# Sixteen small softmax operations of an attention and MLP kernel get a choice of engine, with a new order of the work

## The chip, the cores and the metric

The kernel runs on one core of a Trainium2 chip. The core has five engines that work side by side, each through its own queue in order: TensorE (PE, matrix multiplications and transposes), VectorE (DVE), ScalarE (ACT), GpSimd (POOL) and SyncE (SP), which here only issues transfers. The metric is the device time of one execution in microseconds (us), lower is better.

## The reference

Attention in two parts for 8 batches, 8 heads, 576 positions, 64 channels each, and then an MLP over all 4608 tokens. One part attends within a band of 7 positions, the other between averages of 4 positions; their outputs are added.

```python
q_d = q.reshape(B, H, S // 4, 4, D).mean(axis=3)        # and k_d, v_d alike
out_d = softmax_attention(q_d, k_d, v_d)                # exp(s - max) / (sum + 1e-9)
out_up = np.repeat(out_d, 4, axis=2)
scores = np.where(abs(i - j) < 4, scale * q @ k.T, -1e9)
out_local = softmax(scores) @ v                         # the same 1e-9 beside the sum
x = (out_up + out_local).transpose(0, 2, 1, 3).reshape(B * S, H * D)
h = np.maximum(np.maximum(x @ w1, x @ w2), x @ w3)      # 512 -> 768
return h @ w_out                                        # 768 -> 512
```

Every softmax has two small steps beside its large ones: the maximum is scaled and negated before it goes into the exponential, and 1e-9 is added to the sum before the reciprocal.

## The kernel before, in words

The MLP is most of the work. Its float32 products are made of three TensorE products each: every operand is split into a high part (names in `hi`) and the rest (names in `lo`), and high by high, high by low and low by high are summed. The weights come in six slices of the hidden layer (`whi0`, `wlo0` to `whi5`, `wlo5`, made by `weight_in`), w_out in six parts (`weight_out`). A batch of 512 tokens takes `mlp_in`, which goes through the six slices, and `mlp_out`.

Attention is done by half-batches `n` of four heads. The last 16 pooled positions of each batch are collected as a ninth block. From the third batch on, attention (`block`) runs beside the MLP of earlier batches, mostly on VectorE, ScalarE and GpSimd. For the first two batches (`n` from 0 to 3, the set `DENSE`) there is no MLP to run beside, and `dense` computes the band on TensorE too, in these steps for each half-batch:

- `q`, `v`: loads; `qk` (`pooled_qk`): sums of four positions, `hp` and `qkT` in the profile.
- `s0`, `s1` (`band_scores`): for two heads at a time, scores over windows of 70 positions, a maximum `mx`, eight exponentials on ScalarE that also leave their sums in `z`, then 1e-9 added to `z`, its reciprocal, and the multiplication (`sm`; for n=1 it lies in a tile lent by a weight, `whi`).
- `tail`, `vd`: pooled values (`traw`, `vtail`, `hv`, `vd`).
- `sums` (`pooled_scores`): pooled scores, maximum and its scaling in `nz` (first half, `nm`), six exponentials into `pd` with sums in `nz` (second half, `zd`), 1e-9 added, reciprocal `rd`, multiplication; then `ptld` collects the last positions, TensorE transposes the weights, and copies bring them to `pt` and `ptt`. For n=1 `pd` is lent too and appears as `wlo`.
- `pv`: pooled output (`od`); `v0`, `v1` (`band_values`): TensorE transposes the band weights, copies `y`, 32 products with the values, and the sum with `od` into `t`, which is then split into `xhi` and `xlo` for the MLP.

Nothing of this is issued where it stands in the code. Every operation is recorded (class `Recorder`), with the engines that may take it. `place` then orders all of them: at each turn it takes the engine that can begin first, and on it, among the operations that are ready, the one of smallest priority. Priorities come from tables: `PLAN` for the steps of `dense`, by engine where it matters, `WLOAD` and `WMAKE` for the weights, `WOUT` for w_out, `BEGIN` for the first steps of the fifth half-batch. `HOMES` is a table of letters that ties single copies, multiplications and casts to ScalarE (A) or VectorE (D); "-" leaves the choice to `place`. `emit` issues the result, each engine's list in its order, so all rows of the profile carry its line, L495, and are told apart by their tiles. PSUM has eight banks in two sets, `pm` (three) and `pa` (five); the tile `t` has three buffers, the raw halves of the weights (`hh`, `wo`) two each.

In the kernel before, the two small steps are VectorE's everywhere.

Of the kernel before, what the change touches and what calls it, by code (L numbers as in the profile page):

```python
# [13 lines left out]
AF = mybir.ActivationFunctionType  # L14
# [4 lines left out]
B, H, S, D = 8, 8, 576, 64  # L19
# [11 lines left out]
EPS = 1e-9  # L31
# [1 line left out]
VBUFS = 3  # L33
LAG = 200.0
TAGS = ('pm', 'pm', 'pa', 'pa')
WLOAD = (450.0, 580.0, 2390.0, 260.0, -1745.0, 515.0)
WMAKE = ({"DVE": 1850.0, "ACT": 1125.0}, {"DVE": 560.0, "ACT": -60.0}, {"DVE": 3695.0, "ACT": -1485.0}, {"DVE": 6945.0, "ACT": -1720.0}, {"DVE": 355.0, "ACT": -140.0}, {"DVE": 15.0, "ACT": 40.0})
WOUT = {"DVE": 60.0, "ACT": 2015.0, "SP": 1935.0}
PLAN = (
    (  # L40
        ("q", 0, -2480.0),
        ("v", 0, 905.0),
        ("qk", 0, -2340.0),
        ("s0", 0, {"PE": 1990.0, "DVE": 540.0, "ACT": 1780.0}),
        ("s1", 0, {"PE": -1905.0, "DVE": 65.0, "ACT": 1135.0}),
        ("tail", 0, {"DVE": -405.0, "SP": 480.0}),
        ("q", 1, -975.0),
        ("v", 1, 1150.0),
        ("sums", 0, {"PE": -1675.0, "DVE": -1840.0, "ACT": 260.0}),
        ("vd", 0, {"DVE": -1715.0, "SP": 740.0}),  # L50
        ("qk", 1, -130.0),
        ("s0", 1, {"PE": 15.0, "DVE": -1045.0, "ACT": 1125.0}),
        ("s1", 1, {"PE": 1165.0, "DVE": 235.0, "ACT": 315.0}),
        ("tail", 1, {"DVE": 3360.0, "SP": 2255.0}),
        ("pv", 0, {"PE": -430.0, "ACT": 3475.0}),
        ("v0", 0, {"PE": 195.0, "DVE": -280.0, "ACT": 80.0}),
        ("v1", 0, {"PE": 1795.0, "DVE": 10.0, "ACT": -795.0}),
        ("sums", 1, {"PE": 1905.0, "DVE": 95.0, "ACT": -60.0}),
        ("vd", 1, 3095.0),
        ("pv", 1, {"PE": 95.0, "ACT": 6225.0}),  # L60
        ("v0", 1, {"PE": 1800.0, "DVE": -1230.0, "ACT": 3665.0}),
        ("v1", 1, {"PE": 1685.0, "DVE": 2800.0, "ACT": 1870.0}),
    ),
    (
        ("q", 0, 165.0),
        ("v", 0, -2485.0),
        ("qk", 0, 910.0),
        ("s0", 0, {"PE": 1930.0, "DVE": 60.0, "ACT": 230.0}),
        ("s1", 0, {"PE": 1090.0, "DVE": 1560.0, "ACT": 1425.0}),
        ("tail", 0, {"DVE": 2970.0, "SP": 60.0}),  # L70
        ("sums", 0, {"PE": 820.0, "DVE": -605.0, "ACT": -1890.0}),
        ("vd", 0, {"DVE": -1505.0, "SP": -115.0}),
        ("pv", 0, {"PE": 5.0, "ACT": -1935.0}),
        ("v0", 0, {"PE": 940.0, "DVE": -250.0, "ACT": 1640.0}),
        ("v1", 0, {"PE": 635.0, "DVE": 1895.0, "ACT": 510.0}),
        ("q", 1, 1775.0),
        ("v", 1, 0.0),
        ("qk", 1, -550.0),
        ("s0", 1, {"PE": 615.0, "DVE": -3215.0, "ACT": 130.0}),
        ("s1", 1, {"PE": 225.0, "DVE": 5265.0, "ACT": 485.0}),  # L80
        ("tail", 1, {"DVE": -240.0, "SP": 250.0}),
        ("sums", 1, {"PE": -210.0, "DVE": -120.0, "ACT": 445.0}),
        ("vd", 1, {"DVE": 4855.0, "SP": 1435.0}),
        ("pv", 1, {"PE": -1915.0, "ACT": -2420.0}),
        ("v0", 1, {"PE": 645.0, "DVE": -120.0, "ACT": -85.0, "SP": 6135.0}),
        ("v1", 1, {"PE": 880.0, "DVE": -1450.0, "ACT": 385.0, "SP": 1665.0}),
# [11 lines left out]
DENSE = tuple(range(2 * BANDED))  # L98
# [54 lines left out]
ENGINES = ("PE", "DVE", "ACT", "POOL", "SP")  # L153
DONE_NS = {"PE": 230.0, "DVE": 150.0, "ACT": 190.0, "POOL": 200.0}
MUL_BIAS = {'DVE': 3000.0}
HOMES = {"norm": "AA-A--A-", "band": "A-AADA-AAD-AA---", "hi": "-DAAAAADA-AA", "xhi": "--AA-AAA", "od": "AA--", "pt": "DAAA", "late": "--A-"}
WHEN = {}
PATIENCE = {"PE": 0.0, "DVE": 0.0, "ACT": 0.0, "POOL": 0.0, "SP": 0.0}
LANES = 8
RUN_NS = 200.0  # L160
COLD_US = 35.0
BEGIN = {"PE": 775.0, "DVE": 1695.0, "ACT": 255.0, "POOL": 1095.0, "SP": 510.0}
LAYER_TAGS = {f"{t}{i}" for t in ("whi", "wlo") for i in range(NFT)} | {f"{t}{c}" for t in ("xhi", "xlo") for c in range(NCC)} | {"wo", "hh"}


# [347 lines left out]
def local_global_attention_maxout_kernel(ctx: ExitStack, tc: tile.TileContext, qk_d, qke_d, vw_d, vt_d, wi_d, wo_d, v, ident_d, mask_d, diag_d, band_d, out):  # L513
# [23 lines left out]
    def care(n):  # L537
        return None if n in DENSE else CARE["near" if n < NEAR else "far"]
# [40 lines left out]
    nm, zd = nz[:, 0], nz[:, 1]  # L579
# [60 lines left out]
    def weight_in(ft):  # L640
# [65 lines left out]
    def pooled_scores(n):  # L706
# [7 lines left out]
                    pe.matmul(sps[i][cs, r], qkT[pp, 0, pr, tok : tok + QT], qkT[pp, 1, pr], start=True, stop=True, tile_position=(64 * i, QT * half), skip_group_check=True)  # L714
        for i in range(2):
            dve.tensor_reduce(out=nm[:, i::2], in_=sps[i], axis=AX.X, op=ALU.max)
        dve.tensor_scalar_mul(nm, nm, -1.0 / 128.0)
        pd = st["pd"] if n == 1 else new([P, 6, SD5], tag="pd", name=f"pd_{n}")
        for x in range(6):
            act.activation(pd[:, x, :SD], sps[x % 2][:, x // 2], AF.Exp, bias=nm[:, x : x + 1], scale=1.0 / 128.0, accum_out=zd[:, x : x + 1])  # L720
        dve.tensor_scalar_add(zd, zd, EPS)
        rd = new([P, 6], tag="rd", name=f"rd_{n}")
        dve.reciprocal(rd, zd)

# [5 lines left out]
        pt = st["pt"] = new([P, HH, SD], tag="pt", name=f"pt_{n}")  # L730
# [159 lines left out]
    def band_scores(n, pr, tag):  # L890
        sps = window_scores(n, (pr,), tag, True)[pr]
        if n == 1:
            if pr == 0:
                state[n]["sms"] = guest(n, "sms", "whi4")
            w = 2 * FAC * KWIN
            sm = state[n]["sms"][:, w * pr : w * pr + w].rearrange("p (i u x) -> p i u x", i=2, u=FAC)
        else:
            sm = new([P, 2, FAC, KWIN], tag="sm", bufs=2, name=f"sm_{n}_{pr}")
        mx = new([P, 2, FAC], tag="mx", bufs=2, name=f"mxb_{n}_{pr}")
        z = new([P, 2, FAC], tag="z", bufs=2, name=f"zb_{n}_{pr}")  # L900
        for i in range(2):
# [226 lines left out]
```

## Time and profile before

| | |
|---|---|
| median of 3 runs | 722.41 us (720.45 to 723.44) |
| profiled execution | 720.9 us, its span 719.1 us |
| TensorE busy | 687.1 us, 96% of the span |
| VectorE busy | 533.2 us, 74% |
| ScalarE busy | 400.8 us, 56% |
| GpSimd busy | 184.1 us, 26% |
| mean granted TensorE clock | 0.985 of full |

The span runs from the first to the last instruction of the profiled execution; its own time is 1.8 us longer. "PE MATMUL pm<-xhi_0r,whi_0r" is a TensorE product that writes a bank of `pm` from the tiles behind the arrow. A row of the timeline has start and duration in us, the engine and the operation, and in square brackets how long the engine had stood idle before it and whose result ended that. Where rows are grouped, the last figures are busy us, mean ns of one, and idle time ahead with what ended it. The work of `dense` and of the weights lies in the first 136 us; from 57 us on TensorE has matmuls of the MLP.

### The profile page before, as it was taken

The numbers are of one execution on the slowest core, as the hardware profiler recorded it, in microseconds if no ns is written. First come the engines' busy times: TensorE is split into PE (matmuls) and PEld (weight loads), VectorE is DVE, ScalarE is ACT, GpSimd is POOL, SyncE is SP. The second block draws the span as 40 slices with busy tenths as digits, with TensorE's granted clock in tenths as the row PEclk, the third lists the DMA queues.
The fourth block names the chain that finished last, engine by engine and source line by source line (L and its number), as shares of the span: only waits on it lengthen the run. The fifth ranks groups of instructions, "written<-read, shape, count | busy, mean of one in ns | idle before, by whom it ended". The sixth has DMA issues, their size and how long they took to land.

```text
span 719.1 us, 13533 instructions
## 1 busy us (share of the span) xinstructions
PE 687.1 (96%) x4756; PEld 555.2 (77%) x4756; DVE 533.2 (74%) x952; ACT 400.8 (56%) x1434; POOL 184.1 (26%) x250
## 2 busy tenths in 40 slices
PE   3679999999999999999999999999999999999996
PEld 2557777788878888888888888888888788888885
DVE  6989999887979688869887988796968687431220
ACT  4787774584738283928393739372948387221111
POOL 0000100062415061606150625060605156000000
PEclk9859999999999999999999999999999999999999
DMA  9952717465856677574848684758487673210002
GB/s 361 306 189 84 270 40 219 92 151 139 175 136 191 120 128 185 143 164 81 229 124 187 117 209 113 181 106 184 120 197 130 136 150 78 51 59 30 0 1 58
DMA packets 190817, 101.35 MB, mean 141 GB/s; under 512 B 161454, under 2 KB 166605, under 8 KB 189981
## 3 DMA queue, kind: packets, MB, share of 16 engines
q1 hardware_dynamic: 190749, 100.49, 56.4%
q8 instruction: 37, 0.61, 0.4%
q14 instruction: 31, 0.25, 0.1%
HBM read 71.23 MB, written 29.23 MB: 140 GB/s over the span
## 4 chain that ended last, share of the span: by engine, by line
PE 86%; DVE 7%; DMA 3%; ACT 2%; issue 1%; SPq 0%; ACTq 0%; DVEq 0%
PE pm L495 78%; PE pa L495 8%; DVE pvb L495 1%; DMA pvb<-in_wo_dram 1%; DMA wlo<-in_qk_dram 1%; DVE t L495 1%; DVE hh L495 1%; DVE nz L495 1%; DVE hp L495 1%; SPq L495 0%; DMA t<-xd 0%; DVE xlo_0r L495 0%; ACT pvb L495 0%; DVE mx L495 0%; ACT whi L495 0%
## 5 line engine op out<-in xcount | busy, mean ns | idle before, releaser
L495 PE MATMUL pm<-xhi_0r,whi_0r 128*128 128x512 f32 x648 | 253.9, 392 | 1.5 <-DVE t L495 1.5
L495 PE MATMUL pm<-xlo_0r,whi_0r 128*128 128x512 f32 x648 | 253.4, 391 | 0.0
L495 PE MATMUL pm<-xhi_0r,wlo_0r 128*128 128x512 f32 x648 | 253.3, 391 | 0.0
L495 POOL TENSOR_TENSOR pvb<-v,s 128x256 f32<-128x256 f32 x205 | 161.6, 820 | 203.7 <-DVE s L495 87.3
L495 ACT ACTIVATE pvb<-v,s 128x64 f32<-128x64 f32 x748 | 186.7, 342 | 7.8 <-DMA v<-in_v_dram 3.9
L495 PEld LDWEIGHTS pm<-xhi_0r,whi_0r 128*128 128x128 f32 x648 | 121.6, 188 | 27.7 <-DVE t L495 1.9
L495 PEld LDWEIGHTS pm<-xhi_0r,wlo_0r 128*128 128x128 f32 x648 | 121.7, 188 | 25.8 <-issue 0.6
L495 PEld LDWEIGHTS pm<-xlo_0r,whi_0r 128*128 128x128 f32 x648 | 121.7, 188 | 25.7 <-issue 0.8
L495 DVE TENSOR_TENSOR t<-pm,t 128x512 f32<-128x512 f32 x108 | 74.0, 685 | 81.7 <-PE pm L495 78.7
L495 DVE TENSOR_TENSOR pvb<-pvb 128x768 f32<-128x768 f32 x112 | 107.2, 957 | 5.5 <-POOL pvb L495 2.4
L495 ACT CAST hh_1r<-t 128x512 fp32r<-128x512 f32 x54 | 33.5, 621 | 101.7 <-DVE t L495 101.7
L495 PE MATMUL pm<-wo_0r,hh_1r 128*128 128x512 f32 x216 | 84.1, 392 | 1.4 <-ACT wo_0r L495 1.3
L495 PE MATMUL pm<-wo_1r,hh_1r 128*128 128x512 f32 x216 | 84.9, 393 | 0.0
L495 PE MATMUL pm<-wo_0r,hh_0r 128*128 128x512 f32 x216 | 84.4, 391 | 0.0
L495 ACT ACTIVATE pd<-pa,nz 128x144 f32<-128x144 f32 x90 | 33.2, 382 | 29.3 <-issue 12.6
L495 PEld LDWEIGHTS pm<-wo_0r,hh_1r 128*128 128x128 f32 x216 | 40.5, 188 | 10.9 <-ACT wo_0r L495 1.8
L495 ACT COPY t<-pm 128x512 f32<-128x512 f32 x54 | 31.6, 585 | 30.9 <-PE pm L495 30.9
L495 DVE TENSOR_TENSOR hh_0r<-t,hh_1r 128x512 fp32r<-128x512 f32 x54 | 39.2, 726 | 12.3 <-ACT hh_1r L495 12.2
L495 PEld LDWEIGHTS pm<-wo_1r,hh_1r 128*128 128x128 f32 x216 | 40.6, 188 | 9.8 <-issue 1.0
L495 PEld LDWEIGHTS pm<-wo_0r,hh_0r 128*128 128x128 f32 x216 | 40.6, 188 | 8.4
L495 ACT CAST xhi_0r<-t 128x512 fp32r<-128x512 f32 x30 | 18.7, 622 | 50.5 <-DVE t L495 47.3
L495 ACT COPY y<-pm 128x512 f32<-128x512 f32 (+1 forms) x43 | 23.8, 585 | 25.5 <-PE pm L495 24.8
(139 smaller groups left out, 678.8 us busy)
## 6 DMA issues: line engine op xcount, KB each, us to landing
v<-in_v_dram SPq DMA_DIRECT2D x55, 320.0 KB
qk<-in_qk_dram SPq DMA_DIRECT2D x30, 582.0 KB
out_dram<-y SPq DMA_DIRECT2D x36, 256.0 KB
scr<-sm SPq DMA_DIRECT2D x56, 140.0 KB
xd<-x SPq DMA_DIRECT2D x112, 64.0 KB
t<-xd SPq DMA_DIRECT2D x28, 256.0 KB
wo<-in_wi_dram SPq DMA_DIRECT2D x4, 1536.0 KB
pdd<-pd SPq DMA_DIRECT2D x48, 80.0 KB
```

The source lines that it names most:

```text
L495: getattr(self.engines[o.eng], method)(*map(real, args), **{k: real(x) for k, x in kw.items()})
```

## The change

The two small steps get forms for both engines. `raised` is new: ScalarE adds 1e-9 as the bias of a copying activation, or VectorE adds it as a scalar. `scaled` existed. For the four half-batches of `DENSE`, three new rows of `HOMES` say where they go: "zb" for the eight band sums, "zp" for the four pooled sums, "nm" for the four scaled maxima. With "-" `place` chooses. All later half-batches keep VectorE. The other rows of `HOMES` and all numbers of the priorities are new as well.

```diff
-WLOAD = (450.0, 580.0, 2390.0, 260.0, -1745.0, 515.0)
+WLOAD = (2930.0, -8130.0, 20665.0, -5685.0, -2430.0, 2805.0)
...
-        ("sums", 1, {"PE": 1905.0, "DVE": 95.0, "ACT": -60.0}),
+        ("sums", 1, {"PE": -3880.0, "DVE": 1980.0, "ACT": -7745.0}),
...
-HOMES = {"norm": "AA-A--A-", "band": "A-AADA-AAD-AA---", "hi": "-DAAAAADA-AA", "xhi": "--AA-AAA", "od": "AA--", "pt": "DAAA", "late": "--A-"}
+HOMES = {"zb": "D--A-AA-", "zp": "DA--", "nm": "-A-A", "norm": "AA-A--AD", "band": "---DDA---DD---AD", "hi": "-DAAAA-A-DAA", "xhi": "AA-AADDA", "od": "A-A-", "pt": "D---", "late": "-AA-"}
...
+    def raised(z, engines):
+        forms = {"ACT": [("activation", (z, z, AF.Copy), dict(bias=EPS))], "DVE": [("tensor_scalar_add", (z, z, EPS), {})]}
+        return rec.add(forms, only=engines)
...
-        dve.tensor_scalar_mul(nm, nm, -1.0 / 128.0)
+        scaled(nm, nm, -1.0 / 128.0, homes("nm", n) if n in DENSE else ("DVE",))
...
-        dve.tensor_scalar_add(zd, zd, EPS)
+        raised(zd, homes("zp", n) if n in DENSE else ("DVE",))
...
-        dve.tensor_scalar_add(z, z, EPS)
+        raised(z, homes("zb", 2 * n + pr))
```

In the order that results, 14 of the 16 are ScalarE's (seven on `z`, seven on `nz`); one on each stays with VectorE. Instructions recorded: VectorE 954 before and 931 now, ScalarE 1276 and 1266, GpSimd 255 and 275; TensorE and SyncE keep their numbers. Three places show what is moved.

**VectorE, up to `ptld` of the second half-batch.** `wlo_0_68` (now `wlo_0_69`) is its `pd`, `nz_143` and `rd_193` are its sums and reciprocals, `hh_67` is the raw first weight slice. Before:

```order
L495 TENSOR_TENSOR t_441<-pm_201,od_372 128x512
L495 TENSOR_TENSOR vd_301<-hv_262 128x256
L495 TENSOR_SCALAR nz_143<-nz_143 128x6
L495 TENSOR_TENSOR traw_115<-traw_115 128x64
L495 CAST xhi_0r<-t_441 128x512
L495 RECIPROCAL rd_193<-nz_143 128x6
L495 TENSOR_TENSOR hv_262<-v_141 128x256
L495 TENSOR_TENSOR xlo_0r<-t_441,xhi_0r 128x512
L495 TENSOR_TENSOR wlo_0_68<-wlo_0_68,rd_193 128x2x144
L495 TENSOR_TENSOR ptld_89<-wlo_0_68,rd_193 128x2x32
L495 TENSOR_TENSOR wlo_0_68<-wlo_0_68,rd_193 128x4x128
L495 TENSOR_TENSOR ptld_89<-wlo_0_68,diag_104 128x2x32
```

Now:

```order
L495 TENSOR_TENSOR xlo_0r<-t_437,xhi_0r 128x512
L495 TENSOR_TENSOR vd_298<-hv_256 128x256
L495 TENSOR_TENSOR t_498<-pm_147,od_363 128x512
L495 TENSOR_SCALAR pvb_99<-pvb_99 128x1536
L495 RECIPROCAL rd_193<-nz_143 128x6
L495 TENSOR_TENSOR traw_132<-traw_132 128x64
L495 TENSOR_TENSOR ptld_89<-wlo_0_69,rd_193 128x2x32
L495 RECIPROCAL z_250<-z_250 128x8
L495 TENSOR_TENSOR hv_256<-v_141 128x256
L495 TENSOR_TENSOR xlo_0r<-t_498,xhi_0r 128x512
L495 TENSOR_TENSOR wlo_0_69<-wlo_0_69,rd_193 128x4x128
L495 TENSOR_TENSOR ptld_89<-wlo_0_69,diag_104 128x2x32
```

The small operation on `nz` is gone from VectorE, and so is one of the two multiplications of `wlo`, which is ScalarE's now. A band sum `t_498` and its low part stand ahead of `ptld`, where they stood behind; just above these rows the cast `whi_0r`, the difference `wlo_0r` and a copy `y` have come in as well.

**TensorE at the same place.** `pa_231` and `pa_307` (now `pa_227`, `pa_301`) take the transposes of the pooled weights, `y` by `x` are the 32 band products (fourteen rows of one piece are left out here).

```order
L495 MATMUL pm_147<-y_389,x_177 64x64
L495 MATMUL pm_145<-x_0r,whi_0_72 70x128 x4
L495 MATMUL pa_231<-x_0r,wlo_0_68 128x128 x4
L495 MATMUL pa_307<-x_0r,wlo_0_68 128x128 x2
L495 MATMUL pa_307<-x_0r,ptld_89 128x128
L495 MATMUL pa_307<-diag_104,ptld_89 128x16
L495 MATMUL pm_147<-y_398,x_223 64x64
```

Those rows are of before: the transposes stand behind the first two band products (one to a row half). Now:

```order
L495 MATMUL pm_147<-y_405,x_177 64x64
L495 MATMUL pm_202<-x_0r,whi_0_72 70x128 x4
L495 MATMUL pa_227<-x_0r,wlo_0_69 128x128 x4
L495 MATMUL pa_301<-x_0r,wlo_0_69 128x128 x2
L495 MATMUL pa_301<-x_0r,ptld_89 128x128
L495 MATMUL pa_301<-diag_104,ptld_89 128x16
L495 MATMUL pm_147<-y_389,whi_0_70 64x64
L495 MATMUL pm_145<-x_0r,whi_0_72 70x128 x4
```

The remaining band products and the second set of four transposes of `whi` are done first, and the pooled transposes follow them.

**VectorE, up to the last band sum of the first batch,** `t_441` before, `t_437` now. Before:

```order
L495 RECIPROCAL z_188<-z_188 128x8
L495 TENSOR_REDUCE mx_243<-pa_307 128x4
L495 TENSOR_TENSOR vtail_0_241<-traw_115,diag_104 128x256
L495 TENSOR_TENSOR sm_189<-sm_189,z_188 128x560
L495 TENSOR_REDUCE mx_243<-pa_117 128x4
L495 TENSOR_SCALAR nz_143<-nz_143 128x6
L495 RECIPROCAL rd_193<-nz_143 128x6
L495 TENSOR_TENSOR ptld_89<-pd_175,rd_193 128x2x32
L495 TENSOR_TENSOR t_441<-pm_147,od_372 128x512
```

Now:

```order
L495 TENSOR_TENSOR wlo_0r<-wo_75,whi_0r 128x1536
L495 TENSOR_REDUCE mx_238<-pa_116 128x4
L495 TENSOR_TENSOR t_437<-pm_145,od_363 128x512
L495 TENSOR_REDUCE nz_143<-pa_118 128x3
L495 TENSOR_TENSOR hp_108<-qk_95 128x576
L495 TENSOR_TENSOR qkT_110<-hp_108 128x2x144
L495 TENSOR_REDUCE nz_143<-pa_232 128x3
L495 TENSOR_TENSOR xlo_0r<-t_437,xhi_0r 128x512
```

Operations of the second batch (`hp`, `qkT`, the maxima into `nz`, the normalisation of `sm`, a `ptld`) have gone behind the sum; a weight's low part has come ahead of it.

More of the change, by code (lines that the diff above doesn't have):

```diff
@@ L35 @@
 TAGS = ('pm', 'pm', 'pa', 'pa')
-WLOAD = (450.0, 580.0, 2390.0, 260.0, -1745.0, 515.0)
-WMAKE = ({"DVE": 1850.0, "ACT": 1125.0}, {"DVE": 560.0, "ACT": -60.0}, {"DVE": 3695.0, "ACT": -1485.0}, {"DVE": 6945.0, "ACT": -1720.0}, {"DVE": 355.0, "ACT": -140.0}, {"DVE": 15.0, "ACT": 40.0})
-WOUT = {"DVE": 60.0, "ACT": 2015.0, "SP": 1935.0}
+WLOAD = (2930.0, -8130.0, 20665.0, -5685.0, -2430.0, 2805.0)
+WMAKE = ({"DVE": 5000.0, "ACT": 6610.0}, {"DVE": 3150.0, "ACT": -26960.0}, {"DVE": 23530.0, "ACT": -935.0}, {"DVE": 36010.0, "ACT": -3210.0}, {"DVE": 1710.0, "ACT": -4360.0}, {"DVE": 955.0, "ACT": -5230.0})
@@ L39 @@
+WOUT = {"DVE": -120.0, "ACT": 5770.0, "SP": 6190.0}
 PLAN = (
     (
[L41 to L57, printed above, removed]
-        ("sums", 1, {"PE": 1905.0, "DVE": 95.0, "ACT": -60.0}),
-        ("vd", 1, 3095.0),
-        ("pv", 1, {"PE": 95.0, "ACT": 6225.0}),
@@ L61 @@
-        ("v0", 1, {"PE": 1800.0, "DVE": -1230.0, "ACT": 3665.0}),
-        ("v1", 1, {"PE": 1685.0, "DVE": 2800.0, "ACT": 1870.0}),
-    ),
-    (
[L65 to L76, printed above, removed]
-        ("v", 1, 0.0),
[L78 to L86, printed above, removed]
@@ new lines @@
+        ("q", 0, -10945.0),
+        ("v", 0, 5595.0),
+        ("qk", 0, -9790.0),
+        ("s0", 0, {"PE": -9065.0, "DVE": 3315.0, "ACT": 9330.0}),
+        ("s1", 0, {"PE": -6455.0, "DVE": -470.0, "ACT": 17940.0}),
+        ("tail", 0, {"DVE": -18000.0, "SP": 4150.0}),
+        ("q", 1, -7515.0),
+        ("v", 1, 7525.0),
+        ("sums", 0, {"PE": -1225.0, "DVE": 705.0, "ACT": -8225.0}),
+        ("vd", 0, {"DVE": 2665.0, "SP": 4545.0}),
+        ("qk", 1, -3045.0),
+        ("s0", 1, {"PE": -3490.0, "DVE": -10125.0, "ACT": 2390.0}),
@@ new lines @@
+        ("s1", 1, {"PE": 4485.0, "DVE": 3440.0, "ACT": -8840.0}),
+        ("tail", 1, {"DVE": 8985.0, "SP": 1500.0}),
+        ("pv", 0, {"PE": 15870.0, "ACT": 5015.0}),
+        ("v0", 0, {"PE": -18825.0, "DVE": 700.0, "ACT": -1235.0}),
+        ("v1", 0, {"PE": -11920.0, "DVE": 600.0, "ACT": -9445.0}),
+        ("sums", 1, {"PE": -3880.0, "DVE": 1980.0, "ACT": -7745.0}),
+        ("vd", 1, 3400.0),
+        ("pv", 1, {"PE": -3485.0, "ACT": -2000.0}),
+        ("v0", 1, {"PE": -10245.0, "DVE": -10720.0, "ACT": 9005.0}),
@@ new lines @@
+        ("v1", 1, {"PE": 1600.0, "DVE": 2015.0, "ACT": 4660.0}),
+    ),
+    (
+        ("q", 0, 5.0),
+        ("v", 0, 22255.0),
+        ("qk", 0, -12785.0),
+        ("s0", 0, {"PE": 8280.0, "DVE": 1020.0, "ACT": 4260.0}),
+        ("s1", 0, {"PE": -4985.0, "DVE": 1625.0, "ACT": 4555.0}),
+        ("tail", 0, {"DVE": 4125.0, "SP": 10880.0}),
+        ("sums", 0, {"PE": -3030.0, "DVE": -3420.0, "ACT": -10825.0}),
+        ("vd", 0, {"DVE": -14205.0, "SP": 14455.0}),
+        ("pv", 0, {"PE": -4435.0, "ACT": 27110.0}),
+        ("v0", 0, {"PE": -11725.0, "DVE": -1315.0, "ACT": -7325.0}),
+        ("v1", 0, {"PE": -21105.0, "DVE": 1210.0, "ACT": -1040.0}),
+        ("q", 1, -1135.0),
+        ("v", 1, 0.0),
+        ("qk", 1, 940.0),
+        ("s0", 1, {"PE": -1875.0, "DVE": -9110.0, "ACT": 1630.0}),
+        ("s1", 1, {"PE": -10670.0, "DVE": 7345.0, "ACT": 1210.0}),
+        ("tail", 1, {"DVE": 3535.0, "SP": 6215.0}),
+        ("sums", 1, {"PE": -3055.0, "DVE": -8135.0, "ACT": -12595.0}),
+        ("vd", 1, {"DVE": 25475.0, "SP": 8990.0}),
+        ("pv", 1, {"PE": -3050.0, "ACT": -8995.0}),
+        ("v0", 1, {"PE": -7675.0, "DVE": -8045.0, "ACT": -570.0, "SP": -1620.0}),
+        ("v1", 1, {"PE": -13435.0, "DVE": 9465.0, "ACT": -12600.0, "SP": -11855.0}),
@@ L161 @@
 COLD_US = 35.0
-BEGIN = {"PE": 775.0, "DVE": 1695.0, "ACT": 255.0, "POOL": 1095.0, "SP": 510.0}
+BEGIN = {"PE": -135.0, "DVE": 12930.0, "ACT": -2155.0, "POOL": 2475.0, "SP": -5690.0}
 LAYER_TAGS = {f"{t}{i}" for t in ("whi", "wlo") for i in range(NFT)} | {f"{t}{c}" for t in ("xhi", "xlo") for c in range(NCC)} | {"wo", "hh"}
```

## The prediction

> **What bounds the kernel now.** I read the page first: busy shares and the chain of work that ended last.
>
> ```profile
> span 719.1 us, 13533 instructions
> PE 687.1 (96%) x4756; PEld 555.2 (77%) x4756; DVE 533.2 (74%) x952; ACT 400.8 (56%) x1434; POOL 184.1 (26%) x250
> PE 86%; DVE 7%; DMA 3%; ACT 2%; issue 1%; SPq 0%; ACTq 0%; DVEq 0%
> ```
>
> TensorE (PE) is busy 96% of the span and carries 86% of the chain. So the end is where PE stands when its dense work begins, plus later waits, plus time at a lowered clock. Next, PE's waits, grouped by releaser:
>
> ```profile
> PE pm L495 <- ACT whi L495: 5.4, 3, 4.4
> PE pm L495 <- DVE t L495: 1.5, 1, 1.5
> PE pm L495 <- ACT wo_0r L495: 1.3, 1, 1.3
> ```
>
> The columns are total us, times, longest. After the dense work has begun only the last two kinds count, once each. PE's timeline places them:
>
> ```profile
> 39.86 1.95 PE L495 MATMUL pm<-x_0r,sm 128*70 128x128 f32 x8 [4.36 <-ACT whi L495]
> 43.02 0.48 PE L495 MATMUL pm<-y,x 70*64 70x64 f32 x2 [1.20 <-ACT y L495]
> 43.43 1.07 PE L495 MATMUL pm<-x_0r,whi 128*70 128x128 f32 x4
> 44.29 1.49 PE L495 MATMUL pa<-x_0r,wlo 128*128 128x128 f32 x6
> 46.16 1.97 PE L495 MATMUL pm<-y,x 70*64 70x64 f32 x30
> 48.06 1.07 PE L495 MATMUL pm<-x_0r,whi 128*70 128x128 f32 x4
> 49.06 1.23 PE L495 MATMUL pa<-pt,vd 128*64 128x144 f32 x8
> ...
> 64.32 0.50 PE L495 MATMUL pm<-xhi_0r,whi_0r 128*128 128x512 f32 x1 [1.48 <-DVE t L495]
> ```
>
> PE is dense from 43.02 on. The 1.5 us row is the wait before 64.32, the 1.3 us row lies in the first output layer. Last, the clock, in slices of 3.41 us (TensorE busy, then granted clock, DMA share, GB/s):
>
> ```profile
> 41.56:44.97 3.41, 2.21 (x12) 0.50 0.80 171
> 44.97:48.39 3.42, 3.42 (x39) 0.50 0.21 61
> 48.39:51.80 3.41, 3.41 (x26) 0.50 0.26 84
> 51.80:55.21 3.41, 3.41 (x94) 1.00 0.50 165
> ```
>
> Full speed comes at 51.80, after two slices in which PE never paused. **Idling before that point costs twice**, if it moves the grant: each slice of 3.41 us at half speed loses 1.7 us of work.
>
> **Part 1: the sixteen small operations.** Order says that 14 of the 16 do go to ScalarE (7 `nz` scalings or sums, 7 `z` sums), so the change does what it says. Their prices, with the rows that the other terms need (count, busy us, mean ns):
>
> ```profile
> L495 DVE TENSOR_SCALAR nz<-nz 128x6 f32<-128x6 f32 x32 | 8.1, 253 | 10.1 <-ACT pd L495 9.6
> L495 DVE TENSOR_SCALAR z<-z 128x8 f32<-128x8 f32 x8 | 1.3, 164 | 0.0
> L495 ACT ACTIVATE mx<-mx 128x8 f32<-128x8 f32 x8 | 1.7, 218 | 3.7 <-DVE mx L495 3.7
> L495 DVE TENSOR_TENSOR whi<-whi,z 128x560 f32<-128x560 f32 x1 | 0.7, 731 | 0.0
> L495 DVE TENSOR_TENSOR wlo<-wlo,rd 128x288 f32<-128x288 f32 x1 | 0.4, 447 | 0.0
> L495 DVE TENSOR_TENSOR wlo_0r<-hh,whi_0r 128x1536 fp32r<-128x1536 f32 x2 | 3.5, 1748 | 0.0
> L495 DVE CAST whi_0r<-hh 128x1536 fp32r<-128x1536 f32 x1 | 1.0, 960 | 0.0
> L495 DVE TENSOR_TENSOR xlo_0r<-t,xhi_0r 128x512 fp32r<-128x512 f32 x32 | 22.7, 714 | 2.2 <-ACT xhi_0r L495 1.9
> L495 DVE COPY y<-pm 70x512 f32<-70x512 f32 x1 | 0.7, 677 | 0.0
> L495 DVE CAST xhi_0r<-t 128x512 fp32r<-128x512 f32 x2 | 0.8, 413 | 0.0
> L495 DVE TENSOR_TENSOR hv<-wlo 128x256 f32<-128x256 f32 x2 | 0.8, 410 | 0.0
> L495 DVE TENSOR_SCALAR pvb<-pvb 128x1536 f32<-128x1536 f32 x6 | 5.7, 952 | 0.7 <-ACT pvb L495 0.7
> ```
>
> VectorE (DVE) loses 7 x 0.253 + 7 x 0.164 = 2.9 us; ScalarE (ACT) gains 14 x 0.218 = 3.1 us, priced at its nearest small operation. By itself neither moves the end: it counts only where PE waits. Nor do new waits arise on ACT: the `z` sums stand behind the exponentials that they sum, on the same engine, and an `nz` scaling waits for DVE's maximum with only exponentials queued behind it that need it anyway. The new order decides more.
>
> **Part 2: ScalarE before 43.** Eight multiplications in one row, and two idle times of ACT:
>
> ```profile
> 25.72 2.07 ACT L495 ACTIVATE sm<-sm,z 128x70 f32<-128x70 f32 x8
> ...
> 32.90 0.58 ACT L495 COPY y<-pm 70x512 f32<-70x512 f32 x1 [1.16 <-PE pm L495]
> 36.08 0.38 ACT L495 ACTIVATE wlo<-pa,nz 128x144 f32<-128x144 f32 x1 [2.60 <-DVE nz L495]
> ```
>
> Idle together 3.76 us. Into them go four small operations (0.88) and eight multiplications that normalise `whi` in DVE's place (2.07, the first row): 3.0 of 3.76, so they are hidden. Were they not, each us would lengthen the 39.86 wait in full. Four of the six `wlo` exponentials (0.38 each, the last row) also go behind the `whi` exponentials for which PE waits: up to 1.5 us less ahead of PE. So PE's 39.86 comes about 1.3 us sooner, and with one of the two `y` copies on DVE the 1.20 us wait shrinks: the first band product moves from 43.02 to about 41.3 (bounds 40.4 to 43.0).
>
> **Part 3: the pooled weights of the second half-batch.** This is the main point. On PE their transposes (44.29 before) now stand behind the other 30 band products and four more transposes: 46.16 to 49.06, 2.9 us of work. PE arrives there at 41.3 + 0.41 + 0.86 + 2.9 = 45.5, or 47.2 if it starts at 43.02. They need `ptld` and `wlo` from DVE:
>
> ```profile
> 43.60 0.21 DVE L495 TENSOR_TENSOR ptld<-wlo,diag 128x64 f32<-128x64 f32 x1
> ```
>
> DVE work ahead of that row. Out: three `nz` 0.76, two `z` 0.33, `whi` 0.73, `wlo` 0.45, one cast 0.41, two `hv` 0.82: 3.50. In: `wlo_0r` 1.75, `whi_0r` cast 0.96, `pvb` 0.95, `xlo` 0.71, band sum 0.68 (its row stands in part 4), `y` copy 0.68, one reciprocal 0.2 (an estimate, at the size of `z`): 5.93. Net +2.4, so 46.0 without new waits. One of the added, `xlo`, waits for band products, a sum and ScalarE's cast, all close by: between 0 and 2.3 us; I take the middle, 1.2. So `ptld` is ready at 47.2 (46.0 to 48.3). The transposes take 46.16 - 44.29 = 1.9 and end at 49.1. Before, PE had done the same set of work at 49.06. **Term 0**, with +1.2 and -1.2 as bounds. But PE, there from 45.5, idles 1.7 us inside the slice 44.97 to 48.39.
>
> **Part 4: the 1.48 us wait.** It is for the sum `t` on DVE:
>
> ```profile
> 57.01 0.60 DVE L495 TENSOR_REDUCE nz<-pa 128x3 f32<-128x432 f32 x1
> 57.53 0.75 DVE L495 TENSOR_TENSOR hp<-qk 128x576 f32<-128x576 f32 x1
> 58.31 0.46 DVE L495 TENSOR_TENSOR qkT<-hp 128x288 f32<-128x288 f32 x1
> 63.58 0.68 DVE L495 TENSOR_TENSOR t<-pm,od 128x512 f32<-128x512 f32 x1
> ```
>
> Ahead of it there go away five `nz` 1.27, four `z` 0.66, two of each of the three rows above 3.62, three `hv` 1.23, two normalisations 1.46, `wlo` 0.45, a cast 0.41: 9.1. There come a cast 0.96, a `y` copy 0.68, a larger `pt` copy 0.68 (at the price of `y`), `wlo_0r` 1.75 and another pass over 128x1536 at the same 1.75: 5.8. So at least 3.3 us less: the sum ends by 61.0, and PE asks for it at 64.32 - 1.48 = 62.8. **Term -1.48** (bounds -1.48 to 0, should one more wait stand ahead of it). What is late next is the low part of that sum's tile, five operations (0.60 + 0.75 + 0.46 + 0.60 + 0.71 = 3.1 us) behind, at 64.1. PE takes that tile last, after 64.32 in the trace and 1.7 later here by the clock, less the 1.48: no wait, or 1.0 at most if other waits stand ahead.
>
> **Part 5: the 1.34 us wait in the output layer.** ScalarE's cast there follows DVE's passes over w_out. Through that place DVE loses 2.9 (small operations) and four `hv` 1.6 and `wlo` twice 0.9, and gains a cast 0.96, four copies of 0.68 and two at most as long: 5.0. At least 0.4 less, and nine further small ones (`vtail`, `traw`, `vd`) go to POOL, which has the room at 26%. The loads of w_out stand earlier in SP's queue; none of its other 530 instructions leaves or joins it. **Term -1.0** (bounds -1.3 to 0).
>
> **Part 6: the clock.** If PE's 1.7 us idle spoils the slice 44.97 to 48.39, the two full ones are 48.39 to 51.80 and 51.80 to 55.21, and the grant comes at 55.21: **+1.7**. Bounds: one slice sooner than now (-1.7), two later (+3.4).
>
> The Trainium skill ("TensorE: Matmul & The Clock Gate", What's actually happening) says that one busy window of about 3.4 us opens the gate. By it the gate would have opened at 48.39; the rows above show 0.50 until 51.80, so here the trace disagrees.
>
> **Sum**: 0 - 1.48 - 1.0 + 1.7 = -0.8. The profiled run took 720.9 (span 719.1 and 1.8 around it), so 720.1; the median of the runs, 722.41, lies 1.5 above it: **721.6**.
>
> **Rivals.**
>
> *A, the grant stays at 51.80.* For it: PE may idle less if DVE's bound of 46.0 holds, and what share of busy time suffices no row shows. Against: the slice had no pause at all before. Sum -2.5: 719.9.
>
> *B, faster: the grant comes one slice sooner.* Starting at 41.3, PE would fill 41.56 to 44.97. If one full slice then counts and the gap behind it doesn't, speed comes at 48.39: -2.5 - 1.7 = -4.2, and with the position's -1.2 it is -5.4: 718.2 to 717.0. For it: part 2's idle ScalarE time. Against: the trace's two slices. The Trainium skill's rule on that page, a gate that opens after one busy window, would make this the outcome.
>
> *C, slower: `ptld` misses 48.39.* Its upper bound is 48.3; from 48.4 on the second slice is spoiled too, the grant comes at 58.6: -2.5 + 3.4 + 1.3 of position = +2.2: 724.6. For it: the `xlo` in front waits for a chain over three engines. Against: all its waits must be at their worst.
>
> *D, POOL slows DVE.* Three more POOL operations (`hv`, `vd`) run ahead of `ptld`. What they may cost:
>
> ```profile
> 35.02 1.00 POOL L495 TENSOR_TENSOR traw<-traw 128x128 f32<-128x128 f32 x1 [34.58 <-DMA traw<-in_vt_dram]
> 35.62 0.42 DVE L495 TENSOR_SCALAR nz<-nz 128x6 f32<-128x6 f32 x1
> ```
>
> Beside that POOL operation a small DVE one took 0.42 instead of 0.25: 0.17 each, up to the whole 1.00: 0.5 to 3.0. On the forecast that is 722.1 to 724.6. Against: the small operations have left DVE. The Trainium skill ("SBUF — State Buffer", SBUF: two separate sides) has DVE operations with two inputs and POOL lock each other out for a whole instruction; by it the upper end would hold. The one row here has a single input, so it decides nothing.
>
> **How the numbers follow.** Forecast 0.45 (own range 720.4 to 722.8: the position's bounds), A 0.25, B 0.15, C 0.10, D 0.05. What a measurement can tell from no change is 0.5%, 3.6 us: under 718.8 or over 726.0. Faster: B and a third of A, whose bounds of position and output layer reach 718.4: 0.23. Slower: half of C and of D, where `ptld` is later still: 0.07. Same: 0.70. The range 716.8 to 725.0 leaves out a tenth on either side: B's lower end and C's and D's upper.
>
> **What would show it.** The grant: the first slice at 1.00 begins at 55.2 (A: 51.8, B: 48.4, C: 58.6). The pooled transposes start at 47.2 after a wait for DVE of 1 to 2 us. No wait of 1.5 us for `t` in 60 to 66, and none over 0.5 for `wo_0r`. The 39.86 wait for `whi` at most 3.2 us. It is wrong if ScalarE's small operations show up as releasers of PE, if waits appear between 66 and 135 where there are none now, or if the chain's share on DVE grows beyond 7%.

## The result

The changed kernel is slower, by a little under 1%: 729.08 us median of its first four runs, 1.0093 of the kernel before (95% interval 1.0065 to 1.0121). Three of the four lie between 727.97 and 729.21; the fourth took 2384.98 us and is left out of the ratio. Run again beside the later experiments, the change came out at 1.007 (1.0043 to 1.0098). The prediction was 721.6, with a range of 716.8 to 725.0.

The page of the profile after: span, the busy times, and the granted TensorE clock in 40 equal parts of the span.

```profile
span 726.2 us, 13525 instructions
PE 692.9 (95%) x4756; PEld 559.4 (77%) x4756; DVE 526.3 (72%) x929; ACT 397.3 (55%) x1424; POOL 200.9 (28%) x270
PEclk9858999899999999999999999999999999999999
```

The span is 7.1 us longer, VectorE has 6.9 us less work. The clock, which before was below full only in the first slices, now has a second dent, in the eighth part (127 to 145 us). The waits of TensorE after:

```profile
PE pm L495 <- DVE t L495: 3.9, 1, 3.9
...
PE pa L495 <- DVE wlo L495: 3.1, 1, 3.1
...
PE pm L495 <- ACT whi L495: 0.7, 1, 0.7
```

The waits of 1.48 us (for `t`) and 1.34 us (for `wo_0r`) are gone; a wait of 3.1 us for the pooled weights (`wlo`) and one of 3.9 us for another `t` are new. The timeline of TensorE after places them:

```profile
37.39 1.92 PE L495 MATMUL pm<-x_0r,sm 128*70 128x128 f32 x8 [0.67 <-ACT whi L495]
39.31 0.48 PE L495 MATMUL pm<-y,x 70*64 70x64 f32 x2
...
42.62 1.07 PE L495 MATMUL pm<-x_0r,whi 128*70 128x128 f32 x4
46.80 1.54 PE L495 MATMUL pa<-x_0r,wlo 128*128 128x128 f32 x6 [3.12 <-DVE wlo L495]
...
48.73 0.48 PE L495 MATMUL pm<-y,whi 70*64 70x64 f32 x2
...
130.61 0.39 PE L495 MATMUL pm<-wo_1r,hh_1r 128*128 128x512 f32 x1
...
141.49 0.79 PE L495 MATMUL pm<-wo_1r,hh_1r 128*128 128x512 f32 x1 [3.90 <-DVE t L495]
...
155.46 0.40 PE L495 MATMUL pm<-xhi_0r,whi_0r 128*128 128x512 f32 x1
```

130.61 is the first product of the output layer, 155.46 the first of the second batch. Their like in the kernel before:

```profile
129.86 0.39 PE L495 MATMUL pm<-wo_0r,hh_1r 128*128 128x512 f32 x1
...
149.56 0.39 PE L495 MATMUL pm<-xhi_0r,whi_0r 128*128 128x512 f32 x1
```

So of the 7.1 us only 0.75 had been lost when the output layer began; **5.15 are lost in the output layer of the first batch**, and 1.2 later (three waits of 0.2 us each between 460 and 560 us are new; the rest was not traced). The clock after, in slices of 3.41 us (TensorE busy, then granted clock, DMA share, GB/s):

```profile
45.27:48.68 3.41, 1.88 (x9) 0.50 0.53 160
48.68:52.09 3.41, 3.41 (x25) 0.50 0.04 12
52.09:55.51 3.42, 3.42 (x40) 0.50 0.02 5
55.51:58.92 3.41, 3.41 (x76) 0.50 0.36 98
58.92:62.33 3.41, 3.41 (x39) 1.00 1.01 321
...
137.43:140.84 3.41, 0.16 (x1) 1.00 0.02 1
140.84:144.26 3.42, 2.77 (x7) 0.50 0.00 0
144.26:147.67 3.41, 3.41 (x10) 0.50 0.12 45
147.67:151.08 3.41, 3.41 (x16) 1.00 0.29 109
```

At the front full speed comes at 58.92 instead of 51.80. In the output layer the wait leaves a slice nearly empty, and the clock then stays at half until 147.67. The longer wait (3.90 against 1.34) is 2.56 of the 5.15 us, and half speed from 141.49 to 147.67, which loses at most 3.1, makes up the rest.

Why did TensorE wait there? The same stretch on VectorE:

```profile
133.99 0.68 DVE L495 TENSOR_TENSOR wo_0r<-pvb,wo_1r 128x512 fp32r<-128x512 f32 x1
138.49 0.89 DVE L495 TENSOR_SCALAR pvb<-pvb 128x512 f32<-128x512 f32 x2 [3.82 <-ACT pvb L495]
139.42 1.42 DVE L495 SCALAR_TENSOR_TENSOR pvb<-pvb 128x512 uint32<-128x512 uint32 x2
140.75 0.68 DVE L495 TENSOR_TENSOR t<-pm,t 128x512 f32<-128x512 f32 x1
```

The sum at 140.75 (called so here; it takes the maximum of a product and the earlier ones) frees the bank that TensorE wants at 137.6. What it works on is there long before (the last product of the hidden layer starts at 130.38 and takes 0.39), but the sum stands in VectorE's queue behind four passes over the sixth part of w_out, and these wait for ScalarE's first step on that part, which waits for its load:

```profile
137.80 0.66 ACT L495 ACTIVATE pvb<-pvb 128x512 f32<-128x512 f32 x1 [6.36 <-DMA pvb<-in_wo_dram]
```

SyncE issued that load at 129.05, behind the stores of scores and two value loads:

```profile
124.44 0.75 SPq L495 DMA_DIRECT2D scr<-sm  x1
125.29 3.67 SPq L495 DMA_DIRECT2D v<-in_v_dram  x2
129.05 0.38 SPq L495 DMA_DIRECT2D pvb<-in_wo_dram  x1
```

In the kernel before, the same sum ran as soon as its product had ended, ahead of these passes, and the last part of w_out was in use 3.8 us after the first product of the output layer (133.66 against 129.86), where it is now 7.2 us (137.80 against 130.61):

```profile
130.12 0.69 DVE L495 TENSOR_TENSOR t<-pm,t 128x512 f32<-128x512 f32 x1
...
133.66 0.68 ACT L495 ACTIVATE pvb<-pvb 128x512 f32<-128x512 f32 x1 [0.30 <-DMA pvb<-in_wo_dram]
...
135.96 0.88 DVE L495 TENSOR_SCALAR pvb<-pvb 128x512 f32<-128x512 f32 x2
```

### The profile page after: what moved, and what is told of

Same layout as the page of the kernel before. It is cut to its first block, busy times and chain, and to the rows that moved or that the text cites. A ratio compares the mean times of both kernels' runs of the same rounds, so it can differ in the third digit from the quotient of the medians.

```text
span 726.2 us, 13525 instructions
## 1 busy us (share of the span) xinstructions
PE 692.9 (95%) x4756; PEld 559.4 (77%) x4756; DVE 526.3 (72%) x929; ACT 397.3 (55%) x1424; POOL 200.9 (28%) x270
## 5 line engine op out<-in xcount | busy, mean ns | idle before, releaser
L495 ACT ACTIVATE pvb<-v,s 128x64 f32<-128x64 f32 x724 | 180.9, 341 | 12.2 <-DVE s L495 4.0
L495 DVE TENSOR_TENSOR pvb<-pvb 128x768 f32<-128x768 f32 x112 | 105.7, 944 | 3.9 <-POOL pvb L495 1.6
L495 PE MATMUL pm<-wo_0r,hh_1r 128*128 128x512 f32 x216 | 85.7, 398 | 0.0
L495 PE MATMUL pm<-wo_1r,hh_0r 128*128 128x512 f32 x216 | 85.4, 396 | 0.2 <-DVE hh_0r L495 0.2
L495 PEld LDWEIGHTS pm<-wo_1r,hh_0r 128*128 128x128 f32 x216 | 41.2, 191 | 9.5 <-DVE hh_0r L495 0.6
L495 PEld LDWEIGHTS pm<-wo_0r,hh_1r 128*128 128x128 f32 x216 | 41.3, 191 | 9.3 <-issue 0.6
```

What stands on the lines that cost most here:

```text
L495: getattr(self.engines[o.eng], method)(*map(real, args), **{k: real(x) for k, x in kw.items()})
```

## The experiments

Single executions of one kernel differ by several us: the 31 runs of the kernel before beside the first four experiments lie between 719.3 and 729.75. So verdicts go by the ratio to the kernel before on the same chip; profiles show the mechanism. The theory, L: the order costs the time, by the late load with its queue in the output layer, and the idle time at the front adds to it. The rivals: S, the small operations on ScalarE themselves; Q, VectorE late whatever the load does.

The order was changed behind the planner with one helper, which moves recorded operations (by their number in the program) right behind another one:

```python
def behind(out, at, *seqs):
    ops = [next(o for o in out if o.seq == s) for s in seqs]
    for o in ops:
        out.remove(o)
    k = next(i for i, o in enumerate(out) if o.seq == at)
    out[k + 1 : k + 1] = ops
```

| | ratio to before | 95% interval | median us (before beside it) |
|---|---|---|---|
| change, load first | 0.999 | 0.9966 to 1.0014 | 722.67 (724.07) |
| change, sum first | 1.0027 | 0.9999 to 1.0054 | 724.63 (724.07) |
| change, small operations on VectorE | 1.0074 | 1.0047 to 1.0101 | 729.10 (724.07) |
| before, small operations on ScalarE | 0.999 | 0.9967 to 1.0013 | 722.54 (724.07) |
| change, load first, pooled weights first | 1.0006 | 0.998 to 1.0032 | 722.81 (723.09) |
| change, load first, idle time filled | 0.997 | 0.9943 to 0.9998 | 720.36 (723.09) |
| before, sum late | 1.0045 | 1.002 to 1.007 | 725.23 (723.09) |
| change, load first and sum first | 1.0001 | 0.9969 to 1.0032 | 722.37 (723.09) |
| change, three moves and filled | 0.9964 | 0.9939 to 0.9988 | 719.78 (723.08) |
| before, idle time filled | 1.0026 | 1.0005 to 1.0047 | 724.91 (723.08) |
| change again | 1.007 | 1.0043 to 1.0098 | 728.65 (723.08) |
| three moves, small operations on VectorE | 1.0013 | 0.9991 to 1.0035 | 722.13 (723.00) |
| three moves again | 0.9972 | 0.9958 to 0.9986 | 719.99 (723.00) |

Each also left one profile. Three readings of it, in us: when the full clock came at the front, when the first product of the output layer started, and how long it was from there to the first product of the second batch.

| | full clock from | output layer from | its length |
|---|---|---|---|
| before | 51.80 | 129.86 | 19.70 |
| change | 58.92 | 130.61 | 24.85 |
| change again | 57.58 | 130.33 | 24.04 |
| change, small operations on VectorE | 61.16 | 133.35 | 24.34 |
| change, load first | 51.26 | 128.14 | 19.69 |
| change, sum first | 50.89 | 127.31 | 23.07 |
| change, load first and sum first | 53.30 | 128.51 | 22.38 |
| before, sum late | 52.09 | 130.50 | 22.68 |
| change, load first, idle time filled | 46.82 | 127.30 | 19.45 |
| change, three moves and filled | 47.10 | 126.98 | 18.93 |

The length follows the load and the sum. The first column is another matter: change, change again, load first, sum first, and both together have the same order at the front, and their full clock comes anywhere from 50.89 to 58.92. What the front costs is therefore not a fixed number, and one profile can't give it.

**The load first.** The two value loads go behind the sixth load of w_out.

```diff
+        behind(out, 630, 1034, 1049)   # 630: load of part 6; 1034, 1049: value loads
```

> The changed kernel, with one thing moved: on SyncE the two value loads that stand ahead of the sixth load of w_out go behind it. Theory L (the sixth load, issued at 129.05 and used at 137.80, holds up VectorE, and a sum that frees TensorE's bank stands behind it; the wait of 3.90 us then also drops the clock for 6.8 us): the load is issued about 3 us sooner and the wait falls under 1.5 us with no drop of the clock, 5 us less than the changed kernel, 723 to 725. Rival Q (VectorE is simply late there, whatever the load does): the wait stays above 3 us and the time within 1 us of 729.

The ratio is level with the kernel before (0.999); L had 723 to 725 us, and 722.67 is slightly less. On ScalarE and TensorE:

```profile
132.76 0.67 ACT L504 ACTIVATE pvb<-pvb 128x512 f32<-128x512 f32 x1 [3.79 <-DMA pvb<-in_wo_dram]
```

```profile
136.60 0.50 PE L504 MATMUL pm<-wo_1r,hh_1r 128*128 128x512 f32 x1 [1.48 <-DVE t L504]
```

Counted from the first product of the output layer, the part is used after 4.6 us instead of 7.2; the clock times differ by 5.0 (132.76 against 137.80), but 2.5 of that is an execution whose full clock came sooner. The wait is 1.48 us, with no drop of the clock behind it, and the output layer takes 19.69 us, as in the kernel before:

```profile
128.14 0.39 PE L504 MATMUL pm<-wo_1r,hh_1r 128*128 128x512 f32 x1
...
147.83 0.40 PE L504 MATMUL pm<-xhi_0r,whi_0r 128*128 128x512 f32 x1
```

All of the 5.15 us is back. Q falls.

**The sum first.** The load stays late; the sum goes ahead of the four passes.

```diff
+        behind(out, 881, 632, 633, 634, 635)   # 881: the sum; 632 to 635: passes over part 6
```

> The changed kernel, with one thing moved: on VectorE the sum that frees TensorE's bank (the maximum of the third product of the sixth slice) goes ahead of the four operations on the sixth part of w_out; the load stays as late as it was. Theory L: TensorE goes on for the 15 products of the next bank, 3.4 us, and waits under 2 us for the sixth part instead; with no idle time of a whole slice the clock stays up: 4 to 5 us less than the changed kernel, 724 to 725. Rival Q: no gain over 1 us.

The time is lower, 1.0027 beside 1.007 of the change, though the two intervals touch. It did not come about as L had it: TensorE still waits 3.44 us where under 2 were expected, for another queue, and the clock, which was to stay up, drops for one slice (139.63 to 143.05) where the change loses nearly two. The output layer takes 23.07 us, 1.8 less than in the change. The wait:

```profile
138.17 0.73 PE L504 MATMUL pm<-wo_1r,hh_1r 128*128 128x512 f32 x2 [3.44 <-ACT hh_1r L504]
```

TensorE goes on with the next bank and then waits for ScalarE's cast of that same sum, which stands in ScalarE's queue behind its cast of the sixth part.

**The small operations alone**, both ways. In the order of the change, the 14 stand on VectorE at the same places; in the order of before, on ScalarE.

```diff
+        o = rec.add(forms, only=engines)
+        o.swap = ("DVE", forms["DVE"])   # issued on this engine, at its place in the order
```

> The changed kernel in its own order, but the 14 small operations that it gave to ScalarE stand at the same places on VectorE. Theory N (the order, not the engine of the small operations, costs the time): within 1.5 us of 729, a little slower rather than faster, since VectorE's chain ahead of the pooled weights gets up to 0.8 us longer. Rival S (the small operations on ScalarE cost the time, by longer hand-overs between the engines): 3 to 7 us faster than the changed kernel.

> The kernel before in its own order and with its own table of engines, but the same 14 small operations stand at the same places on ScalarE. Theory N: within 1.5 us of the kernel before, 721 to 723.5, perhaps 1 us less, as VectorE loses 2.9 us ahead of the waits of 1.48 and 1.34 us. Rival S: 3 us slower or more.

1.0074 beside 1.007 of the change itself, and 0.999 beside 1: in either order the engine of these operations doesn't move the time by what these runs can tell, some 0.4% for the first pair and 0.2% for the second. S, with at least 3 us, falls by the second; the order costs the time.

**The sum late in the kernel before**, the reverse test. With it go what needs the sum (its cast and low part) and the first products of the next bank.

```diff
+        behind(out, 635, 881, 882, 883, 924, 925, 926)
```

> The kernel before, with one thing moved: on VectorE the sum that frees TensorE's bank in the output layer goes behind the last passes over the sixth part of w_out, as the change has it. Theory L: TensorE's wait there grows from 1.3 to about 4.5 us, and with a whole idle slice the clock drops: 3 to 6 us slower than the kernel before. Rival Q (that place has slack): within 1 us.

It is slower by 0.45% (some 3 us), at the lower end of L. The wait is smaller than expected, in two pieces of 0.86 and 1.91 us, the second for the sum:

```profile
139.61 0.50 PE L504 MATMUL pm<-wo_0r,hh_1r 128*128 128x512 f32 x1 [1.91 <-DVE t L504]
```

The clock dropped all the same (slices: TensorE busy, then clock):

```profile
137.46:140.87 3.41, 1.50 (x7) 1.00 0.00 0
140.87:144.29 3.42, 3.42 (x10) 0.51 0.00 0
144.29:147.70 3.41, 3.41 (x17) 1.00 0.36 138
```

**Both moves.**

> The changed kernel with both moves, the sixth load of w_out sooner and the sum ahead of that part's passes. Theory L: the wait of 1.48 us that e1_load_first still shows at the sum goes, 1 to 1.5 us less than e1_load_first; if the part itself is then late, no gain.

No gain over the load alone: TensorE waits 2.75 us for ScalarE's cast `hh_1r`, queued as in the second experiment, the clock drops for one slice, and the output layer of the profile takes 22.38 us. The sum alone in front is not enough; its cast has to come with it.

**The front: pooled weights first.** Work that the pooled weights don't need goes behind their transposes on VectorE and ScalarE.

```diff
+        behind(out, 197, 179, 118, 214, 152)              # 197: ptld; 179: band sum; 214: copy y
+        behind(out, 179, 180)
+        behind(out, 219, 285, 293, 275, 286, 181, 287, 288)   # raw weights, wlo_0, a low part
```

> The changed kernel with its sixth w_out load ahead of two value loads (as in e1_load_first), and at the front VectorE's and ScalarE's work that the pooled weights of the second half-batch don't need (the low part of the first weight slice, two low parts of band sums, passes over raw weights) put behind the transposes of these weights. Theory G (TensorE's 3.1 us of idle time ahead of 46.8 costs its own length, and more where it delays the clock): the idle time is gone, TensorE stands 2 to 3 us further, 3 to 5 us less than e1_load_first, a ratio of 0.992 to 0.996 to the kernel before. Rival H (the idle time is paid back later anyway, since TensorE then waits for the sums and low parts that were put off): no gain over 1 us.

The idle time of 3.1 us is gone, and the gain with it, as rival H says. TensorE now arrives earlier at the MLP and waits there for what was put off:

```profile
56.59 0.51 PE L507 MATMUL pm<-xhi_0r,whi_0r 128*128 128x512 f32 x1 [3.18 <-DVE xhi_0r L507]
57.91 0.51 PE L507 MATMUL pm<-xlo_0r,whi_0r 128*128 128x512 f32 x1 [0.81 <-DVE xlo_0r L507]
```

The clock tells the same: in this profile full speed came at 41.62, some ten us sooner than with the load alone, but the two waits left so little in two slices (1.55 and 1.29 us of 3.41) that the next one, 58.69 to 62.10, ran at half speed again. The cast `xhi_0r` that TensorE waits for starts on VectorE at 55.59 here and at 55.80 with the load alone: VectorE has the same work to do up to there, and it sets the pace, whichever part of it TensorE meets first.

**The front: idle time filled,** with transposes in the change, with band products in the kernel before.

```diff
+        again = [o for o in out if o.seq in (215, 216, 217, 218)]   # 128-row transposes, three times more
+        k = out.index(again[-1])
+        out[k + 1 : k + 1] = again * 3
...
+        again = [o for o in out if 134 <= o.seq <= 149]             # before: 64x64 products, twice more
+        k = next(i for i, o in enumerate(out) if o.seq == 149)
+        out[k + 1 : k + 1] = again * 2
```

> As e1_load_first, but TensorE repeats the last four transposes ahead of its idle time three times (3 us of extra work at half clock, which rewrites the same values), so that it is busy until the pooled weights come. Its position doesn't change; only the clock can. If idle time ahead of 46.8 delays the grant of the full clock, the grant comes a slice or more sooner and the time is 1.5 to 3 us less than that of e1_load_first. If what counts is what the slices behind it hold, the time is the same, or up to 1 us longer.

> The kernel before, with its idle time of 4.36 us ahead of 39.86 filled: TensorE does the 32 band products that it has just done twice more, 4 us at half clock, with the same values written. If idle time ahead of the dense work delays the grant of the full clock whatever the work is, the grant comes one slice or two sooner: 1.5 to 3 us less than the kernel before. If such products of 64 by 64 don't count for the clock, the time is the same.

Useless work in idle time gained perhaps 0.2% in the one (0.997 beside 0.999 of the load alone, intervals that overlap) and nothing in the other (1.0026, if anything slower). The clock is clearer than the time. In the changed kernel the grant comes between 46 and 47:

```profile
45.00:46.00 1.00, 1.00 (x7) 0.50 0.81 191
46.00:47.00 1.00, 0.75 (x4) 0.59 0.66 233
47.00:48.00 1.00, 0.69 (x6) 1.00 0.61 157
```

All four profiles with this filling have it between 46.82 and 48.01, the five with the same order at the front and no filling between 50.89 and 58.92. In the kernel before, filled, it came at 51.42, hardly sooner than without (51.80):

```profile
44.43:47.84 3.41, 3.41 (x40) 0.50 0.25 72
47.84:51.25 3.41, 3.41 (x25) 0.50 0.29 86
51.25:54.66 3.41, 3.41 (x82) 0.97 0.39 112
```

The two fillings differ in kind (128 rows against 64) and in place (up to the dense work, or with a gap of 1.2 us behind), so which of these decides is not shown.

**A version that beats both.** Load first, sum first, ScalarE's cast of the sum ahead of its cast of the part, and the filled idle time:

```diff
+        behind(out, 630, 1034, 1049)
+        behind(out, 881, 632, 633, 634, 635)
+        behind(out, 882, 636)                # 882: cast of the sum; 636: cast of part 6
```

> The changed kernel with the sixth w_out load sooner, with VectorE's sum ahead of the passes over that part, with ScalarE's cast of that sum ahead of its cast of the part (in e8_load_and_sum TensorE waited 2.75 us for the first, queued behind the second), and with the idle time at the front filled by repeated transposes as in e6_filled. Theory L with the clock: no wait over 1.5 us in the output layer and the clock stays up there, 1 to 1.5 us less than e6_filled, 718.5 to 720, a ratio of 0.993 to 0.996 to the kernel before. If the part itself is now what TensorE waits for, no gain over e6_filled.

0.9964, and 0.9972 when run again: faster than the kernel before in both, by 0.3%, and 1.1% faster than the change beside it. The wait in the output layer is down to 0.85 us, and the layer takes 18.93:

```profile
135.27 0.73 PE L509 MATMUL pm<-wo_1r,hh_1r 128*128 128x512 f32 x2 [0.85 <-ACT wo_1r L509]
```

> The changed kernel as it is, beside the others of this call: 1.0065 to 1.0121 of the kernel before, by its first runs, 728 to 731; the grant of the clock between 50 and 62, differing from execution to execution by whole slices of 3.41 us.

The change came out at 1.007, as expected; its profile has the same two waits (3.12 and 3.39 us), and a clock that drops in the output layer again.

**And the small operations in that version?** The last pair differs in nothing else.

> As e9_three_moves, but with the 14 small operations at the same places on VectorE. In the order of the change VectorE's chain ahead of the pooled weights gets 0.6 to 0.8 us longer (three scalings or sums of 0.25 us), and the two kernels differ in nothing else. Theory N: 0 to 1.5 us slower than e9_three_moves, 719.5 to 721.5, 0.996 to 0.999 of the kernel before. If the small operations are worth more than their length on VectorE, 2 us slower or more; if ScalarE's share cost something, faster than e9_three_moves.

> The kernel of e9_three_moves again, beside the other of this call: 0.994 to 0.999 of the kernel before.

1.0013 (0.9991 to 1.0035) against 0.9972 (0.9958 to 0.9986): on ScalarE they are worth 0.4%, 2.1 us by the medians. Theory N, with 1.5 us at most, missed; the other case of the expectation, 2 us or more, came about. In the profiles TensorE reaches the pooled weights sooner with them; on VectorE it waits 1.49 us where it waits 0.67 us with them on ScalarE:

```profile
39.13 1.92 PE L510 MATMUL pm<-x_0r,sm 128*70 128x128 f32 x8 [1.49 <-ACT whi L510]
```

```profile
38.40 2.09 PE L509 MATMUL pm<-x_0r,sm 128*70 128x128 f32 x8 [0.67 <-ACT whi L509]
```

At the first product of the MLP the two profiles differ by 0.64 us, at the second batch by 1.2, and their spans by only 0.2 (719.3 and 719.1), so where the difference of the medians arises is not shown.

## Why the prediction was wrong, step by step

- **Part 5 failed, and with it the forecast.** Its term was -1.0; the output layer measured +5.15 (and +4.3 in the profile of the change run again). It counted VectorE's work up to that place, rightly less, and took w_out's loads to stand earlier on SyncE. The sixth stands later, behind two value loads. Nor did it ask what else is queued on VectorE behind that part: not only the part was late, but the sum that frees a bank of TensorE. What the load alone cost, the first experiment shows: without its delay the output layer takes as long as before, and the change is level with the kernel before. The prediction's own signs of error looked for new waits between 66 and 135 us; this one began at 137.6.
- **It also priced a wait at its length only.** Part 6 counted idle time that delays the full clock at the front; that idle time can take the clock away again once it is there, no term had. In the output layer this cost up to 3.1 us of the 5.15.
- **Part 6 can't be called right.** It put the grant at 55.21 and the price at +1.7. In the profile after, it came at 58.92, 7.12 us later than before, which is +3.6 at half speed. In four more profiles with the same order at the front it came at 50.89, 51.26, 53.30 and 57.58, and so from 0.9 us sooner to 7.1 later than in the profile before: a term between -0.5 and +3.6. The idle time that the part reasoned from is 3.1 us in all five. What sets the grant it did not have, and these runs do not show it.
- **Part 3 held by number.** The pooled transposes were put at 47.2 (46.0 to 48.3), and started at 46.80; their end, with the whole set of work, 48.73 against 49.06 before, term -0.3. But 1.2 of the 47.2 were for a wait of VectorE that did not come: its rows from 29.3 to 46.8 show none, and its work took that time instead. So the agreement is partly luck. TensorE's idle time ahead was 3.12, not 1.7, because TensorE arrived at 43.7 instead of 45.5.
- **Part 2 was right in kind and too small.** 39.86 was to come 1.3 us sooner; it came at 37.39, 2.5 sooner, and the wait for `whi` fell from 4.36 to 0.67. The first band product, put at 41.3 (40.4 to 43.0), started at 39.31, outside these bounds.
- **Part 4 held:** the wait of 1.48 us is gone and none took its place there.
- Up to the output layer these terms give 3.6 - 1.5 - 0.3 = +1.8 in the profile after, its rows show +0.75; the remaining 1.0 of gain was not traced. In the five profiles named above, the output layer begins between 2.5 us sooner and 0.75 later than before.
- **Part 1** said that the engine of the small operations moves the end only where TensorE waits for it. In the old order their move gained 0.1% (0.999, interval to 1.0013), nothing that can be told from zero. In the order of the change the pair (1.0074 beside 1.007) can't tell 0.4% from nothing. With the output layer mended and the idle time filled they are worth 0.4%.
- **Rivals.** A, the grant at 51.80, did not come about in the change's profile, but nearly so in those of the load first and the sum first (51.26 and 50.89); no rival named the output layer, where the time was lost. B, the grant at 48.4, came about in none of the five. C named the grant at 58.6 and a time of 724.6, but by another way: `ptld` did not miss 48.39, so its closeness to 58.92 is luck. D: GpSimd ran nothing between 35.3 and 47.4, the stretch ahead of `ptld`, so it could not have slowed VectorE there.
- The sentence of the Trainium skill ("TensorE: Matmul & The Clock Gate", What's actually happening), one busy window opens the gate, failed at the front as the prediction said, here by more (three full slices at 0.50 in the profile after). In the output layer it held: one full slice of 128x512 products (144.26 to 147.67) was enough. At the front it did both: with the load first, the full slice from 41.02 to 44.43 was not enough, the one from 47.85 to 51.26 was.

## What to carry to other kernels

Where a change reorders queues, follow every load whose landing gates a step, past each transfer now ahead of it, and then list what stands behind the waiting instruction on its engine: the price is that of the most urgent thing in that list. A long wait of TensorE has a second price: in the output layer here, waits of 2.75 us and more, and two that came to 2.77 together, were followed by at least a slice at half speed, 1.7 us of lost work, and single waits of up to 2.1 us (in the kernel before with its idle time filled) were not. It belongs in the sum wherever such a wait can arise. Work taken off a busy engine is worth something only where TensorE is waiting for that engine. And when a clock step differs from execution to execution, one profile says what happened in it, not what the change costs: compare the length of a stage, as the output layer here, or many runs.

## What the runs showed of the hardware

- A slice of 3.41 us need not be idle for the clock to drop: 1.50 us of TensorE work in it did not hold it (137.46 to 140.87 in the kernel before with the sum late), nor did 1.46 (136.22 to 139.63 with the sum first). In the same profile 1.92 us did (132.81 to 136.22), and 1.55 us did with the pooled weights first (51.86 to 55.28).
- Fully busy slices need not bring the clock back at once: at the front it came after three in a row in the change and the change again, after two in the kernel before, and after one with the load first and the sum first; one of 128x512 products was enough in the output layer. The slices at the front hold transposes and products of 64 rows or 64 columns, but the kind of work alone does not settle it. With the load first, the slice from 47.85 to 51.26, and in the change again the one from 47.34 to 50.75, hold nearly the same rows of the same order, both fully busy and both behind a slice with 0.3 us of work. Full speed followed the first at once; the second was followed by two more slices at half speed. What decides stays open.
- The load of 512 KB took 8.75 us from issue to use (129.05 to 137.80) behind score stores and value loads, and 7.45 with the value loads behind it (its issue began at 125.31 and took 2.12, its use at 132.76). How much of either is waiting behind other transfers was not separated.
